# A low-rank product in transposed form, laid out by a DMA transpose, in a Fourier mixing and MLP kernel

## The chip, the cores and the metric

The kernel runs on one core of one Trainium2 chip. The time is the device time of one execution in microseconds (us); before the change it was measured in three runs. A core has five engines, each with its own instruction stream: TensorE (PE in the profile; PEld is its weight loads), VectorE (DVE), ScalarE (ACT), GpSimd (POOL) and SyncE (SP), which here issues DMAs only. TensorE multiplies a stationary operand ("weights", loaded by an instruction of its own) with a moving operand and writes to PSUM; ScalarE and VectorE move results from PSUM to SBUF.

## The reference

x has 8 batches of 3136 rows (n) and 256 columns (d). First the real part of a Fourier transform along both axes, then a low-rank mix along the rows and an MLP along the columns:

```
X   = real(fft(fft(x, axis=1), axis=2))          # (8, 3136, 256)
h   = X.transpose(0, 2, 1) @ U @ V               # U 3136 x 32, V 32 x 3136
u   = X + h.transpose(0, 2, 1)
out = u + relu(u @ w_ch1) @ w_ch2                # w_ch1 256 x 1024, w_ch2 1024 x 256
```

## The kernel before

Everything is kept with d on the partitions (two halves of 128, index `s`) and rows n along the free axis. The Fourier transform is done by folding x with its mirror images on VectorE (`fold`) and multiplying with cosine and sine tables on TensorE (`transform`, tiles `pt`, then `pst`). It yields the two halves of the transformed columns as `ST[b]["S"]` and `ST[b]["T"]`. Rows n and 3136 - n come from the same numbers with the two column halves exchanged, so only half of the rows, 1568 a batch, are walked explicitly.

These 8 x 1568 columns are cut into 25 chunks (`c`) of 512, across batch bounds; `pieces(c)` gives the batches in a chunk. For each chunk:

- `front(c, hf)`: the low-rank part `ph` (TensorE) plus S and T (VectorE) gives `u`, for the direct rows (hf 0) and the mirrored rows (hf 1). SyncE then issues a DMA transpose of `u` into `ut`, which is used when the output is put together; GpSimd makes small corrections `fx` from it.
- `direct(c, q)`: for four blocks j of the hidden layer, w_ch1 times u into four PSUM tiles `p1`; ScalarE applies relu and writes `h`.
- `mirrors(c, q)`: the same four PSUM tiles are turned into the hidden layer of the mirrored rows, without a full product. Two terms are added: `WD` (difference of the halves of w_ch1) times `uo` (S - T), and the low-rank term, `QF` times `DV` (difference of the direct and mirrored columns of V). Then relu again.
- `second_product(c, hf, t0)`: w_ch2 times `h`; VectorE adds `ut`, GpSimd adds `fx`, and `store` issues the DMA out.

`QF` is what the change is about. `lowrank(b)` computes the transform of the batch's product with U, as `ptt`; copies of it go to `TA` and `TX`, and for batches 1 to 7 SyncE issues a DMA transpose of `TX` into `TD[b % 2]` (L659). `TD` has d on the partitions, two halves s, and 128 columns: the 32 rank columns four times over. `hidden(b, hh)` multiplies it with w_ch1 (`W1`), with TD as the weights, 512 columns of the hidden layer at a time (L689):

```
mm(pt[:], TD[b % 2][:, s, :], W1[:, s, hh * CH:(hh + 1) * CH], start=(s == 0), stop=(s == 1))
nc.scalar.copy(QF[b % 2][:, hh * CH:(hh + 1) * CH], pt[:])
```

So `QF[b % 2]` is 128 x 1024: on each of the four groups of 32 partitions the same 32 x 1024 product. `mirrors` (L795) needs it so: each of its four blocks g takes its weights from partition group g, and the four matmuls of 32 rows run on four row groups of TensorE.

Batch 0 is prepared in the setup, with a transposed product on TensorE (`transposed`) in place of the DMA transpose, and its two calls of `hidden` (L1038, L1082) use a spare PSUM tile.

What sets the order: the main loop runs over the chunks and has six slots in each (`turn(c, 0)` to `turn(c, 5)`); the steps of the next batch's transform are put into slots by `transform(b)` (L857 to L881) and `put`. The matmuls, and the folds on VectorE, stay in the order of the program; the scheduler places the other engines' instructions. For batch 1 the list ends `rank + ch, q`: in one slot the low-rank product and the four `chan` steps, in the next (the last of chunk 2) both halves of `hidden`. Batch 1 begins in chunk 3, at column 32 of it. For batch 2, `q` takes the last two slots of its list; for later batches each step has its own slot, and the two halves of `hidden` are the last two of 15, the last of them in the last slot before the chunk in which the batch begins. In that chunk `mirrors(c, 0)` is the first to read the new `QF`.

Of the kernel before, what the change touches and what calls it, by code (L numbers as in the profile page):

```python
# [10 lines left out]
BF16 = mybir.dt.bfloat16  # L11
FP32 = mybir.dt.float32
# [4 lines left out]
P = 128  # L17
# [14 lines left out]
def kernel(  # L32
# [9 lines left out]
    nc = tc.nc  # L42
    B, S, D = x.shape
    R = moe_U.shape[1]
    H = moe_w_ch1.shape[1]
    JT = H // P
    HALF = S // 2
    CH = 512
# [3 lines left out]
    cpool = ctx.enter_context(tc.tile_pool(name="cpool", bufs=1))  # L52
    psum = ctx.enter_context(tc.tile_pool(name="psum", bufs=1, space=bass.MemoryType.PSUM))
# [51 lines left out]
    BUFS = {"dft": 2, "p1": 4, "p2": 2}  # L105
# [15 lines left out]
    def iota(out_, pattern, base, m=0):  # L121
# [8 lines left out]
                      in_=bass.AP(moe_U.tensor, moe_U.offset + R,  # L130
                                  [[NI * R, PQ], [784 * R, 4], [1, NI * R]]))
# [54 lines left out]
    W1 = cpool.tile([P, 2, H], BF16, name="w1")  # L186
# [3 lines left out]
    DV = cpool.tile([P, HALF], BF16, name="dv")  # L190
# [1 line left out]
    TA = [cpool.tile([P, 256], BF16, name=f"ta{s}", tag=f"ta{s}") for s in range(2)]  # L192
    TX = cpool.tile([P, 256], BF16, name="tx")
    TD = [cpool.tile([P, 2, P], BF16, name=f"td{s}", tag=f"td{s}") for s in range(2)]
    QF = [cpool.tile([P, H], BF16, name=f"qf{s}", tag=f"qf{s}") for s in range(2)]
    MSN = cpool.tile([P, 256], BF16, name="msn")
    MC = cpool.tile([P, 256], BF16, name="mc")
    MSX = cpool.tile([P, 256], BF16, name="msx")
# [251 lines left out]
    def mm(*a, **k):  # L450
        ins = nc.tensor.matmul(*a, **k)  # L451
        if len(pinned) > 1:
            tc.keep_in_program_order(ins)
        if pinned:
            pinned.append(ins)
# [68 lines left out]
    def seq(b, par, typ, pn, tag="dft", part=True):  # L524

        d = state(b)
        ne = NE if b else 0
        pt = psum.tile([P, QW], FP32, tag=tag, name="pt", bufs=BUFS[tag])
        d["pt"] = pt
        todo = products(b, par, typ, P * typ, pn == 1, ne)  # L530
        if typ == 0:
            todo = todo + products(b, par, 1, 256, (pn == 1) == (par == 1), ne)
        add_up(pt, todo)
        if pn == 0:
            ev = d["ev"] = wp.tile([P, QW], FP32, tag="ev", name="ev", bufs=EB)
            w = (2 * NT if par else TE) + ne
            nc.scalar.copy(ev[:, :w], pt[:, :w])
            if part:
                apart(b, par)
# [12 lines left out]
    def join(b, par, typ, kept=None, low=True, high=True):  # L552

        d = kept or ST[b]
        ne = NE if b else 0
        pt, ev = d["pt"], d["ev"]
        dst = ST[b]["A"] if typ == 1 else ST[b]["B"]
        p_, e_ = pt[:, 0:2 * NT], d["eh"][:]
        up, dn = dst[:, 1176:784:-1], dst[:, 1177:HALF + 1]
        if low:  # L560
            nc.vector.tensor_tensor(up, p_, e_, op=AL.add)
        if not high:
            return
        if typ == 1:
            nc.vector.tensor_tensor(dn, e_, p_, op=AL.subtract)
        else:
            nc.vector.tensor_tensor(dn, p_, e_, op=AL.subtract)
        if ne:
            pu, eu = 2 * NT, NT
            nc.vector.tensor_tensor(ST[b]["tab"][:, typ, par, :].rearrange("p (g r) -> p g r", r=R),  # L570
                                    four(pt, pu), four(ev, eu), op=AL.add)

    def even_rows(b, typ, pn, tag="dft"):

        d = state(b)
        ne = NE if b else 0
        if pn == 0:
            d["pe"] = psum.tile([P, QW], FP32, tag=tag, name="pt", bufs=BUFS[tag])
        pt = d["pe"]
        todo = products(b, 0, typ, P * typ, pn == 1, ne)  # L580
        if typ == 0:
            todo = todo + products(b, 0, 1, 256, pn == 0, ne)
        for n, (at, w, rhs) in enumerate(todo):
            mm(pt[:, at:at + rhs.shape[-1]], w, rhs, start=(pn == 0 and n == 0),
               stop=(n == len(todo) - 1), skip_group_check=True)
        if pn == 0:
            ev = d["ve"] = wp.tile([P, QW], FP32, tag="ev", name="ev", bufs=EB)
            nc.scalar.copy(ev[:, :TE + ne], pt[:, :TE + ne])
            return
        dst = d["A"] if typ == 1 else d["B"]  # L590
        nc.scalar.copy(strip(dst[:], 392, [[-2, NT + 1]]), pt[:, 0:NT + 1])
        nc.scalar.copy(strip(dst[:], 391, [[-2, NT]]), pt[:, NT + 1 + ne:TE + ne])
        if ne:
            nc.scalar.copy(d["tab"][:, typ, 0, :].rearrange("p (g r) -> p g r", r=R), four(pt, TE - NT))
# [7 lines left out]
    def mirrored(b, typ, kept):  # L602

        ne = NE if b else 0
        pt, ev = kept["pe"], kept["ve"]
        dst = ST[b]["A"] if typ == 1 else ST[b]["B"]
        nc.vector.scalar_tensor_tensor(strip(dst[:], 394, [[-1, 2], [2, NT]]),  # L607
                                       strip(ev[:], 1, [[NT + ne, 2], [1, NT]]), 2.0 if typ else -2.0,
                                       strip(pt[:], 1, [[NT + ne, 2], [1, NT]]),
                                       op0=AL.mult, op1=AL.subtract if typ else AL.add)  # L610
# [71 lines left out]
                   stop=(typ == 1))  # L682
        nc.scalar.copy(TD[b % 2][:], pt)

    def hidden(b, hh, spare=None):

        pt = spare or psum.tile([P, CH], FP32, tag="dft", name="pq", bufs=BUFS["dft"])
        for s in range(2):
            mm(pt[:], TD[b % 2][:, s, :], W1[:, s, hh * CH:(hh + 1) * CH], start=(s == 0), stop=(s == 1))  # L689
        nc.scalar.copy(QF[b % 2][:, hh * CH:(hh + 1) * CH], pt[:])  # L690

    def width(c):
        return min(CH, NCOL - c * CH)
# [1 line left out]
    def pieces(c):  # L695

        cuts = []
        r = c * CH
        while r < c * CH + width(c):
            b, n = divmod(r, HALF)  # L700
            end = min(c * CH + width(c) - b * HALF, HALF)
            cuts.append((b, n, end, r - c * CH))
            r = b * HALF + end
        return cuts
# [60 lines left out]
    def extent(c, hf):  # L765
        return width(c) + (B if hf == 0 and width(c) < CH else 0)
# [17 lines left out]
    def mirrors(c, q):  # L784

        k = CK[c]
        w = extent(c, 1)
        for g in range(4):
            j = 4 * q + g
            mm(k["p1"][g][:, :w], WD[:, j * P:(j + 1) * P], k["uo"][:, :w], start=False, stop=False,  # L790
               skip_group_check=True)
        for b, lo, hi, col in pieces(c):
            for g in range(4):
                j, rows = 4 * q + g, slice(g * R, (g + 1) * R)
                mm(k["p1"][g][:, col:col + hi - lo], QF[b % 2][rows, j * P:(j + 1) * P], DV[rows, lo:hi],  # L795
                   start=False, stop=True, skip_group_check=True)
        for g in range(4):
            nc.scalar.activation(k["h", 1][q][:, g, :w], k["p1"][g][:, :w][:, ::-1], AF.Relu)  # L798
# [58 lines left out]
    def transform(b):  # L857

        def odd_rows(typ, pn):
            seq(b, 1, typ, pn)  # L860
            if pn:
                join(b, 1, typ)

        def even(typ, pn):
            even_rows(b, typ, pn)
            if pn:
                mirrored(b, typ, ST[b])

        a = [lambda pn=pn: even(1, pn) for pn in range(2)]
        s = [lambda pn=pn: even(0, pn) for pn in range(2)]  # L870
        c = [lambda pn=pn: odd_rows(1, pn) for pn in range(2)]
        d = [lambda pn=pn: odd_rows(0, pn) for pn in range(2)]
        rank = [lambda: lowrank(b)]
        ch = [lambda ch=ch, h=h: chan(b, ch, h) for ch in range(2) for h in range(2)]
        q = [lambda hh=hh: hidden(b, hh) for hh in range(2)]
        if b == 1:
            return 11, [a[:1], a[1:] + c[:1], c[1:], [s[0], d[0]], [s[1], d[1]], rank + ch, q]
        if b == 2:
            return 23, [a[:1], a[1:] + c[:1], [], c[1:] + s[:1], s[1:], d[:1], d[1:], rank, ch[:1], ch[1:3],
                        ch[3:], q[:1], q[1:]]  # L880
        return 6 * (b * HALF // CH) - 15, [[x] for x in a + c + d[:1] + s + d[1:] + rank + ch + q]  # L881

    CK = {}
    ST = {}
# [146 lines left out]
    spare = psum.tile([P, CH], FP32, tag="p2", name="spare", bufs=BUFS["p2"])  # L1031
# [3 lines left out]
    nc.vector.tensor_tensor(WD[:], W1[:, 1, :], W1[:, 0, :], op=AL.subtract)  # L1035
    nc.gpsimd.memset(WD[0:1], 0.0)
    first_rows(0, 0, "dft")
    hidden(0, 0, spare)  # L1038
    setup.close()
    cp = ctx.enter_context(tc.tile_pool(name="cp", bufs=2))  # L1040
    front(0, 0)
# [37 lines left out]
    direct(0, 0)  # L1079
    chan(0, 2, 0)  # L1080
    chan(0, 2, 1)
    hidden(0, 1, spare)  # L1082
    mirrors(0, 0)
    front(0, 1)
    first_rows(0, 256, "p2")
# [4 lines left out]
    chan(0, 3, 1, "p2")  # L1090
    along_d(OD, xr, EOR_, 1)
    mirrors(0, 1)
    front(1, 0)
    alone(EV, xr, EOR_)
# [8 lines left out]
    for c in range(1, NCH):  # L1103
# [17 lines left out]
        if c + 1 < NCH:  # L1121
# [6 lines left out]
                      in_=CK[NCH - 1]["o", 0][:B, 2, :])  # L1128
# [32 lines left out]
```

## Time and profile before

| what | us |
|---|---|
| median of three runs | 456.95 |
| lowest, highest run | 455.19, 462.61 |
| profiled execution, its own time | 455.13 |
| its span, first to last instruction | 453.0 |
| TensorE matmul busy | 434.7 |
| VectorE, ScalarE, GpSimd busy | 314.5, 298.5, 121.5 |
| `pq` matmuls (the product `hidden`, batches 1 to 7), 28 of them, mean of one 0.379 | 8.2 |
| `qf` copies on ScalarE, 14 of them, mean of one 0.587 | 8.1 |

All numbers below the second line come from one profiled execution. In a timeline a row gives the start, the length, the engine, the line, and output<-inputs by tile name; the line of a matmul is that of the helper `mm` (L451), so matmuls are told apart by their tiles. A matmul's length contains its drain, which overlaps with the next one, so the price of a group of matmuls is read from its start to the start of what follows. `[idle before <-releaser]` at a row's end is the engine's idle time before it and what ended it. Rows of SyncE (SPq) give the time that the queue spent on issuing a DMA, not the time until the data landed; that is read from who waited for it, or from the completion marks in the trace, 16 for each transfer.

### The profile page before, as it was taken

How to read it: one execution, taken by the hardware profiler on the slowest of the kernel's cores; microseconds unless marked ns; L12 is line 12 of the kernel's file. 1: busy time of each engine (PE TensorE's matmuls, PEld its weight loads, DVE VectorE, ACT ScalarE, POOL GpSimd, SP SyncE). 2: the span in 40 equal slices, each digit the busy share in tenths (PEclk: the TensorE clock that was granted, in tenths of full speed). 3: DMA queues.
4: the chain of work that ended last, by engine and by line, in shares of the span. 5: the costliest groups of instructions: out<-in, count | busy, mean ns of one | idle time of the engine just before them, and what ended most of it. 6: DMA issues, size and time to landing. Idle time of an engine off the chain costs nothing.

```text
span 453.0 us, 9053 instructions
## 1 busy us (share of the span) xinstructions
PE 434.7 (96%) x3351; PEld 285.4 (63%) x3351; DVE 314.5 (69%) x639; ACT 298.5 (66%) x640; POOL 121.5 (27%) x338
## 2 busy tenths in 40 slices
PE   5989999999999999999999999999999999999995
PEld 2664666566666676667666666667666666666673
DVE  8898975995887768669667768579667444344442
ACT  7958755766567657765667657775667657765751
POOL 8970221341224224422133111321122000111010
PEclk9999999999999999999999999999999999999999
DMA  7996797769467683946878397774325423435463
GB/s 205 221 224 150 180 238 103 170 165 239 121 169 212 155 199 84 261 105 156 170 147 209 99 188 91 147 197 128 94 75 131 104 72 98 94 112 121 117 128 107
DMA packets 89132, 67.79 MB, mean 150 GB/s; under 512 B 55372, under 2 KB 82400, under 8 KB 89088
## 3 DMA queue, kind: packets, MB, share of 16 engines
q1 hardware_dynamic: 83608, 52.86, 51.3%
q0 software_dynamic: 5472, 14.36, 12.7%
q8 instruction: 26, 0.43, 0.4%
q14 instruction: 18, 0.15, 0.1%
q10 hardware_dynamic: 8, 0.00, 0.0%
HBM read 28.86 MB, written 25.69 MB: 120 GB/s over the span
## 4 chain that ended last, share of the span: by engine, by line
PE 84%; DVE 7%; DMA 4%; ACT 2%; issue 1%; SPq 1%; POOL 0%; DVEq 0%; POOLq 0%
PE p L451 64%; PE pt L451 10%; PE pst L451 4%; DMA xr<-in_x_dram 3%; PE ph L451 3%; PE pq L451 1%; DVE eof L446 1%; DVE u L737 1%; DVE A L607 1%; DVE eor L446 1%; PE ptt L451 1%; DVE go L446 1%; DMA out_dram<-o 1%; SPq L87 1%; DVE eos L446 0%
## 5 line engine op out<-in xcount | busy, mean ns | idle before, releaser
L451 PE MATMUL p<-w,h 128*128 128x256 bf16 x1576 | 189.1, 273 | 0.0
L451 PEld LDWEIGHTS <-h 128*128 128x128 bf16 x1576 | 149.6, 98 | 39.2 <-issue 17.4
L798 ACT ACTIVATE h<-p 128x512 bf16<-128x512 f32 (+1 forms) x200 | 101.6, 594 | 59.4 <-PE p L451 57.3
L782 ACT ACTIVATE h<-p 128x512 bf16<-128x512 f32 (+1 forms) x200 | 101.8, 600 | 7.3 <-PE p L451 7.3
L850 DVE TENSOR_TENSOR o<-p,ut 128x256 f32<-128x256 f32 x95 | 40.0, 421 | 91.4 <-PE p L451 72.8
L451 PE MATMUL p<-u,w 128*128 128x512 bf16 (+1 forms) x400 | 93.2, 375 | 0.6 <-DVE u L737 0.6
L855 POOL TENSOR_TENSOR o<-o,fx 128x2 f32<-128x2 f32 (+1 forms) x95 | 34.7, 365 | 135.0 <-DVE o L851 68.0
L451 PEld LDWEIGHTS <-w 128*128 128x128 bf16 x400 | 38.9, 98 | 39.8 <-issue 2.1
L451 PE MATMUL p<-uo,wd 128*128 128x512 bf16 (+1 forms) x200 | 50.8, 374 | 0.2
L57 POOL DMA_INDIRECT xf<-in_x_dram,xidx x32 | 38.7, 1210 | 20.8 <-DVE eof L446 9.6
L446 DVE TENSOR_TENSOR eor<-xr 99x1016 bf16<-99x1016 f32 x32 | 38.4, 1209 | 1.6 <-DMA xr<-in_x_dram 1.6
L851 DVE TENSOR_TENSOR o<-p,ut 128x256 f32<-128x256 f32 x95 | 39.3, 413 | 0.0
L446 DVE TENSOR_TENSOR eof<-xf 99x1016 bf16<-99x1016 f32 x32 | 38.2, 1208 | 0.2 <-issue 0.2
L737 DVE TENSOR_TENSOR u<-ph,T 128x512 bf16<-128x512 f32 (+8 forms) x64 | 35.0, 558 | 4.5 <-PE ph L451 2.8
L737 DVE TENSOR_TENSOR u<-ph,S 128x512 bf16<-128x512 f32 (+8 forms) x64 | 35.0, 558 | 0.9 <-PE ph L451 0.3
L755 POOL TENSOR_TENSOR fx<-ut 128x4 f32<-128x4 bf16 x48 | 11.7, 243 | 68.9 <-DMA ut<-u 68.9
L451 PEld LDWEIGHTS <-wd 128*128 128x128 bf16 x200 | 19.4, 97 | 16.7 <-issue 0.4
L754 POOL TENSOR_TENSOR fx<-ut 128x4 f32<-128x4 bf16 x24 | 6.6, 273 | 77.8 <-DMA ut<-u 72.5
L451 PE MATMUL pt<-te,gc 98*128 98x229 bf16 (+1 forms) x192 | 24.2, 260 | 1.8 <-DVE u L737 1.6
L451 PEld LDWEIGHTS <-go 98*128 98x128 bf16 x216 | 19.2, 97 | 10.2 <-issue 3.1
L645 ACT CAST T<-pst 128x392 bf16<-128x392 f32 (+1 forms) x28 | 17.4, 621 | 11.5 <-PE pst L451 11.5
L451 PEld LDWEIGHTS <-gc 98*128 98x128 bf16 x216 | 19.2, 97 | 6.4 <-issue 2.2
(167 smaller groups left out, 465.9 us busy)
## 6 DMA issues: line engine op xcount, KB each, us to landing
out_dram<-o SPq DMA_DIRECT2D x33, 512.0 KB
xr<-in_x_dram SPq DMA_DIRECT2D x16, 784.0 KB
out_dram<-o SPq DMA_DIRECT2D x8, 384.0 KB
out_dram<-o SPq DMA_DIRECT2D x9, 256.0 KB
out_dram<-o SPq DMA_DIRECT2D x8, 128.0 KB
ut<-u SPq DMA_TRANSPOSE x48
vv<-vv SPq DMA_DIRECT2D x3, 196.0 KB
out_dram<-o SPq DMA_DIRECT2D x6, 96.0 KB
```

What stands on the lines that cost most here:

```text
L57: nc.gpsimd.indirect_dma_start(out_, None, bass.AP(t.tensor, t.offset, [[w, rows], [1, w]]), bass.IndirectOffsetOnAxis(idx, 0), element_of ...
L446: ins = nc.vector.tensor_tensor(*a, **k)
L451: ins = nc.tensor.matmul(*a, **k)
L645: nc.scalar.copy(to, pt[:, :n])
L737: nc.vector.tensor_tensor(u[:, s, at:at + hi - lo], phs[s][:, at:at + hi - lo], src, op=AL.add)
L754: nc.gpsimd.tensor_tensor(fx[:, :, 0], ut[:, n:2 * n, 0], ut[:, 0:n, 0], op=AL.subtract)
L755: nc.gpsimd.tensor_tensor(fx[:, :, 1], ut[:, 0:n, 0] if hf else ut[:, n:2 * n, 0], ut[:, n + 1:2 * n + 1, 0], op=AL.subtract)
L782: nc.scalar.activation(k["h", 0][q][:, j - 4 * q, :w], p1[:, :w], AF.Relu)
L798: nc.scalar.activation(k["h", 1][q][:, g, :w], k["p1"][g][:, :w][:, ::-1], AF.Relu)
L850: nc.vector.tensor_tensor(o[:, ts, 0:P], p2[:, :w, 0:P], ut[:rows, ts, 0:P], op=AL.add)
L851: nc.vector.tensor_tensor(o[:, ts, P:D], p2[:, :w, P:D], strip(ut[:rows], (CH // P + t0 + 1) * P, [[P, w], [-1, P]]), op=AL.add)
L855: nc.gpsimd.tensor_tensor(o[:, ts, cols], o[:, ts, cols], fx[:rows, ts, 1 - hf:], op=AL.add)
```

## The change

For batches 1 to 7 the product is computed the other way round. `W1` gives the weights, block by block of 128 hidden columns, and the moving operand is the first of the four copies in `TD`, 32 columns. Eight blocks and two halves s make 16 matmuls into one PSUM tile of 128 x (8 x 32). One ScalarE copy puts it into `QT` (128 x 256), and one DMA transpose on SyncE's queue turns its two blocks of 128 x 128 into `QF[b % 2]`, now 128 x 2 x 128: block j = 4q + g lies on partition group g, at q. Each product is thus held once instead of four times. Batch 0 keeps the wide product (`hidden_0`) with a tile of its own, `QF0`, laid out by q, g, column. `mirrors` takes its weights from the one or the other. In the list of steps the product is now one step: in the same slot for batch 1, and ahead of the last `chan` steps for the others (ahead of one step of two for batch 2, ahead of two for batches 3 to 7, whose lists have 14 steps instead of 15).

```diff
-    QF = [cpool.tile([P, H], BF16, name=f"qf{s}", tag=f"qf{s}") for s in range(2)]
+    QF0 = cpool.tile([P, 2, 4, P], BF16, name="qf")
+    QF = [cpool.tile([P, 2, P], BF16, name=f"qf{s}", tag=f"qf{s}") for s in range(2)]
+    QT = cpool.tile([P, 2 * P], BF16, name="qt")
...
-    def hidden(b, hh, spare=None):
-
-        pt = spare or psum.tile([P, CH], FP32, tag="dft", name="pq", bufs=BUFS["dft"])
+    def hidden_0(hh, pt):
+
         for s in range(2):
-            mm(pt[:], TD[b % 2][:, s, :], W1[:, s, hh * CH:(hh + 1) * CH], start=(s == 0), stop=(s == 1))
-        nc.scalar.copy(QF[b % 2][:, hh * CH:(hh + 1) * CH], pt[:])
+            mm(pt[:], TD[0][:, s, :], W1[:, s, hh * CH:(hh + 1) * CH], start=(s == 0), stop=(s == 1))
+        nc.scalar.copy(QF0[:, hh].rearrange("p g m -> p (g m)"), pt[:])
+
+    def hidden(b):
+
+        pt = psum.tile([P, JT, R], FP32, tag="dft", name="pq", bufs=BUFS["dft"])
+        for j in range(JT):
+            for s in range(2):
+                mm(pt[:, j, :], W1[:, s, j * P:(j + 1) * P], TD[b % 2][:, s, 0:R], start=(s == 0), stop=(s == 1))
+        nc.scalar.copy(QT[:], pt[:].rearrange("p j r -> p (j r)"))
+        nc.sync.dma_start_transpose(out=QF[b % 2][:], in_=QT[:])
...
-                j, rows = 4 * q + g, slice(g * R, (g + 1) * R)
-                mm(k["p1"][g][:, col:col + hi - lo], QF[b % 2][rows, j * P:(j + 1) * P], DV[rows, lo:hi],
+                rows = slice(g * R, (g + 1) * R)
+                mm(k["p1"][g][:, col:col + hi - lo], QF0[rows, q, g, :] if b == 0 else QF[b % 2][rows, q, :], DV[rows, lo:hi],
...
-        q = [lambda hh=hh: hidden(b, hh) for hh in range(2)]
+        q = [lambda: hidden(b)]
...
-                        ch[3:], q[:1], q[1:]]
-        return 6 * (b * HALF // CH) - 15, [[x] for x in a + c + d[:1] + s + d[1:] + rank + ch + q]
+                        q, ch[3:]]
+        return 6 * (b * HALF // CH) - 15, [[x] for x in a + c + d[:1] + s + d[1:] + rank + ch[:2] + q + ch[2:]]
...
-    hidden(0, 0, spare)
+    hidden_0(0, spare)
...
-    hidden(0, 1, spare)
+    hidden_0(1, spare)
```

## The prediction

> **What bounds the kernel now.** I read the page first (share of the engines, chain of waits), then TensorE's timeline around the product that is changed, then the queue of SyncE and the landings of its transposes, then the granted clock by windows.
>
> ```profile
> span 453.0 us, 9053 instructions
> PE 434.7 (96%) x3351; PEld 285.4 (63%) x3351; DVE 314.5 (69%) x639; ACT 298.5 (66%) x640; POOL 121.5 (27%) x338
> PE   5989999999999999999999999999999999999995
> PE 84%; DVE 7%; DMA 4%; ACT 2%; issue 1%; SPq 1%; POOL 0%; DVEq 0%; POOLq 0%
> ```
>
> TensorE is busy in nearly every slice and carries 84% of the chain of waits. Its timeline shows no idle stretch over 0.1 us after 150 us, and only six over 0.2 us between 60 and 150 us. So time taken off TensorE's stream comes off the end one for one, and so does a wait put into it.
>
> The product that is changed, and what reads it, at the first batch that it touches (batch 1), in TensorE's timeline (start, duration, what):
>
> ```profile
> 84.44 1.03 PE L451 MATMUL pq<-w,td 128*128 128x512 bf16 x4
> 85.30 1.89 PE L451 MATMUL p<-u,w 128*128 128x512 bf16 x8
> 90.40 0.41 PE L451 MATMUL p<-dv,qf 32*128 32x32 bf16 x8
> ```
>
> The next product starts 0.86 us after the four wide matmuls, so that is their price (the 1.03 contains a drain that overlaps). The last line is the first use of batch 1's `qf` (eight matmuls: four narrow ones of batch 0, from 90.44 four of batch 1): 5.96 us after the product began.
>
> **The matmuls.** Seven batches (1 to 7) change; batch 0 keeps its form (`hidden_0`). Removed: 4 matmuls of 512 columns, 0.86 us a batch. Added: 16 of 32 columns, each with its own 128-column weight load. The nearest row is the low-rank product of the setup, also 32 columns on 128-column weights:
>
> ```profile
> 26.36 0.35 PE L451 MATMUL ptu<-te,gc 98*128 98x32 bf16 x8
> ...
> 26.77 0.35 PE L451 MATMUL ptu<-te,gc 98*128 98x32 bf16 x8
> ...
> 27.17 0.85 PE L451 MATMUL pt<-te,gc 98*128 98x197 bf16 x8
> ```
>
> 32 such matmuls stand between 26.36 and 27.17: 25 ns each, so 16 take 0.40 us. A farther row bounds it from above: the `pu` matmuls, with weights only 98 columns wide, run 12 in 0.54 us (12.28 to 12.82), 45 ns each, 0.72 us for 16. From below 0.40 is the fastest in the trace. I take 0.40: same width of weights. Gain 0.46 us a batch, 3.2 us in all (1.0 us at the other bound).
>
> [...]
>
> **The evictions.** ScalarE loses two `qf` copies of 0.586 us and gets one of 128x256: 0.37 us by the `tx` copy of the same shape. ScalarE is 66% busy and idles 0.4 to 1.2 us ahead of those copies; no gain on the path, no loss. One bank of the two-buffer `dft` pool is taken per batch instead of two; the trace has no wait for it at this place: nothing.
>
> **The transposes.** Seven transposes of 128x256 go on SyncE's queue. Their shape is that of `td<-tx` (1.17 to 1.97 us of queue time). Behind them wait the x loads and output stores of that stage; the folds that read those loads come at least a chunk (some 16 us) later, so 1.2 us there costs nothing. What matters is when they land, since TensorE now waits for them at the mirror products. Landing is not instant, even when issued at once: by the trace's completion marks (last of 16) `td` landed 2.3, 2.4, 2.7, 3.6, 4.1, 2.3 and 2.3 us after the start of its issue. In six of the seven a `ut` transpose was still in flight when `td` was issued, and `td` always landed after it, by 0.26 to 0.55 us in the three slow ones (177.58 then 178.13; 228.90 then 229.16; 282.96 then 283.44): the queue hands on in order.
>
> In the changed program each new transpose stands right behind a `ut` transpose on SyncE, except for batch 2, where two small loads lie between. At batch 1:
>
> ```profile
> 84.49 5.36 SPq L751 DMA_TRANSPOSE ut<-u  x1
> 89.90 0.43 SPq L87 DMA_DIRECT2D xr<-in_x_dram  x1
> ```
> ```profile
> 96.43 0.54 POOL L755 TENSOR_TENSOR fx<-ut 128x4 f32<-128x4 bf16 x1 [6.39 <-DMA ut<-u]
> ```
>
> The first view is SyncE's queue, the second is GpSimd. SyncE is held by this `ut` transpose until 89.85, while 784 KB of x, a 512 KB store and two gathers are in the queues (DMA share 0.91 from 84 to 97 us); the transpose's data are complete at 96.35 (marks of 14 engines by 95.45), which is when GpSimd goes on. The new transpose issues at 89.9, so its bounds are: 92.2 if it lands 2.3 us after issue as on an idle queue, 96.6 to 96.9 if it lands behind the `ut` one. I take 96.7, by those three rows. TensorE comes to its use at 90.44 - 0.46 = 89.98. All that is queued behind is TensorE itself, in program order: the mirror products, the next low-rank products and second products, and with them every eviction. It resumes at 96.7 against 90.44: **+6.3 us** (the first 0.46 is swallowed).
>
> Some of it is absorbed. VectorE was itself late there (it evicts the next `ph` at 92.24 although the product ended at 91.0), so the gaps of 0.22 and 0.53 us that TensorE has at 93.1 and 101.2, the second waiting on VectorE, close: -0.8. Bounds: 0, and -2.1 if the later gaps at 120.0 (0.87) and 145.7 (0.46) close too.
>
> Batches 2 to 7, TensorE's need against the landing that I expect, in the old times: batch 2 142.8 against 135.3; batch 3 194.3 against 189.0; batch 4 245.1 against 239.8; batch 5 296.06 - 0.46 = 295.6 against 295.06 + 0.4 = 295.5; batches 6 and 7 over 9 us spare. No wait, but batch 5 has none to spare: 0, bound +0.5.
>
> **The earlier place.** From batch 2 on the product moves ahead of chan steps, so `td` is needed sooner: in batch 5 at 282.62 (where the third `chan` stood) instead of 286.76, and `td` landed there at 283.44: +0.8 (0 to 1.3). In the other batches `td` is 2.6 us or more early.
>
> **The clock.** A stop of 6.7 us has a price of its own:
>
> ```profile
> 444.00:452.80 8.80, 3.60 (x32) 2.55 (x29) 1.99 (x6) 0.22 (x1) 1.09 (x6) 1.00 0.37 122
> 452.90:453.00 0.10, 0.00 (x0) 0.00 (x0) 0.00 (x0) 0.00 (x0) 0.00 (x0) 0.50 0.00 0
> ```
>
> The windows give TensorE's granted clock third from the end: 1.00 up to 452.8, then 0.50. The last matmul ends at 447.60 and the clock record falls at 452.87: 5.3 us of rest halve it. At the start the first matmul is at 5.23 and full clock is recorded from 9.14: 3.9 us to come back. A stop of 6.7 us is longer than 5.3, so I count half speed over 3.9 us: +1.9 (0 if the stop is cut under 5.3).
>
> [...]
>
> **Sum.** +6.3 - 6 x 0.46 (2.8) + 1.9 + 0.8 - 0.8 = +5.4 us on the profiled execution, whose own time is 455.13 (span 453.0, 2.1 around it): 460.5. The median of the three runs is 456.95, 1.8 above; on that footing I forecast **461.5**, 1.0% slower.
>
> **Rivals.**
> *The wait stays short.* If the new transpose lands at 92.2, TensorE resumes 1.8 us late, the clock holds, and +1.8 - 2.8 + 0.4 (half of batch 5's) - 0.4 gives -1.0: 455.9. If nothing waits anywhere, -3.2: 453.7. For it: `td` lands 2.3 us after issue four times of seven. Against: no `td` landed before a `ut` transpose that was in flight ahead of it. Chance 0.17.
>
> *The wait repeats (slower).* Place: batch 5's mirror product. Its `ut` transpose took 7.4 us from issue to landing; the ones issued at 62.37 and 84.49 took 11.9. If, with work bunched behind the first stop, batch 5's takes 11.9 as well, `qf` lands at 300.0 against 295.6: +4.4, with the clock's 1.9 another 6.3 at most, so 466.7 to 468.6; batches 3 and 4 would join once theirs land 5.2 us later. It decides from 3.7 us of further wait, since 2% is 9.1 us. For it: no margin in batch 5, and waits of this queue double under load. Against: by then stores and loads are steady. Chance 0.24.
>
> *The narrow matmuls are slower than 25 ns.* At 45 ns, 7 x 0.32 = +2.2: 463.7. [...] Chance 0.06.
>
> *It gains over 2%.* The four wide matmuls of seven batches total 6.0 us (1.3%); even free they don't reach 9.1. Chance 0.02, for something that I don't see.
>
> The forecast itself has 0.51, with its own range 458 to 464.5. The range that leaves out no more than 2 in 10 goes from 453.7 (nothing waits) to 468.6 (the repeat). Faster or slower by over 2%, about what runs of this kernel can tell (455.19 to 462.61 before), is 447.8 and 466.1: faster 0.02; slower 0.25, the repeat and a little of the slow matmuls; the rest, 0.73, within.
>
> **What would show it.** In the changed profile: the 16 matmuls at 25 ns (about 0.4 us to the next product); an idle stretch of TensorE of about 6.7 us ahead of `p<-dv,qf` near 90 us, ended by the DMA of `qf`; a granted clock under 1.00 for some 4 us after it; no such stretch before 280 us; a short one near 282 us, ended by `td`. I am wrong if `qf` lands well before 95 us, if the same stretch comes back in batches 3 to 5, or if the clock stays whole through the stop.

## The result, and the profile after

The changed kernel takes 463.69 us (median of five runs, 461.22 to 465.37) against 456.93 for the kernel before on the same chip. The ratio is 1.0145, with an interval of 1.0104 to 1.0186: about 1.5% slower. The profiled execution took 463.69 us.

The page of the changed kernel, the lines that answer to those of before (span; busy times; TensorE and its granted clock in 40 slices; the chain of waits):

```profile
span 461.8 us, 9236 instructions
...
PE 434.9 (94%) x3435; PEld 286.6 (62%) x3435; DVE 314.3 (68%) x639; ACT 294.2 (64%) x633; POOL 125.9 (27%) x338
...
PE   5989999739999999999999999999999999999995
...
PEclk9999999959999999999999999999999999999998
...
PE 86%; DMA 6%; DVE 4%; ACT 2%; SPq 1%; issue 1%; DVEq 0%; POOLq 0%
```

TensorE's row has two slices that are not full, 7 and 3, and the clock's row a 5 in the second of them. Everything else looks as before. The span grew by 8.8 us, and one place holds more than that. TensorE's timeline there, and further on, at batches 2 and 5:

```profile
84.25 0.55 PE L453 MATMUL pq<-td,w 128*128 128x32 bf16 x16
84.66 1.89 PE L453 MATMUL p<-u,w 128*128 128x512 bf16 x8
...
89.75 0.19 PE L453 MATMUL p<-dv,qf 32*128 32x32 bf16 x4
99.47 0.59 PE L453 MATMUL p<-dv,qf 32*128 32x480 bf16 x4 [9.53 <-DMA qf<-qt]
...
100.42 3.54 PE L453 MATMUL p<-w,h 128*128 128x256 bf16 x16
...
148.64 1.67 PE L453 MATMUL p<-u,w 128*128 128x512 bf16 x7 [0.27 <-DVE u L747]
...
293.17 0.56 PE L453 MATMUL pq<-td,w 128*128 128x32 bf16 x16 [0.61 <-DMA td<-tx]
```

The sixteen narrow matmuls cost 0.41 us (84.25 to 84.66), against 0.86 before. At 89.75 the four matmuls of batch 0 run from `QF0`; the next four, the first of batch 1, wait 9.53 us for the transposition. The 16 second products behind them take 3.54 us instead of 1.9. SyncE's queue shows what came before:

```profile
84.30 6.33 SPq L761 DMA_TRANSPOSE ut<-u  x1
90.72 1.19 SPq L700 DMA_TRANSPOSE qf<-qt  x1
```

By the completion marks `ut` landed at 98.98 and `qf` at 99.43: issued at 90.72, it took 8.7 us. The windows of the stage (columns: stretch; its length; busy time of PE, PEld, DVE, ACT and POOL; granted clock; DMA share; GB/s):

```profile
84.00:93.50 9.50, 5.95 (x56) 3.75 (x54) 7.57 (x12) 3.97 (x8) 1.51 (x2) 1.00 1.01 203
93.60:103.70 10.10, 4.22 (x24) 2.58 (x25) 1.55 (x6) 2.07 (x4) 1.80 (x6) 0.50 0.75 141
103.90:110.00 6.10, 6.10 (x48) 3.58 (x46) 5.05 (x9) 3.63 (x8) 3.53 (x6) 1.00 0.65 176
```

The clock is 0.50 from 93.5 to 103.8, the last 4.3 us of it after TensorE has resumed, and the DMA engines are full (share 1.01) up to 93.5. TensorE's list of waits gives the new transposition once only:

```profile
PE p L453 <- DMA qf<-qt: 9.5, 1, 9.5
...
PE pq L453 <- DMA td<-tx: 0.6, 1, 0.6
```

To see where the rest went, the start of each mirror product (its first `p<-uo,wd` matmul) was compared between the two traces. After minus before, in us:

| from | to | after minus before | what lies there |
|---|---|---|---|
| start | batch 1's product | -0.18 | |
| batch 1's product | the stop | -0.65 | the product, -0.46 |
| the stop | batch 2's product | +10.68 | +11.33: 9.53 idle, the rest clock |
| batch 2's use | batch 3's product | +10.74 | the gain of batch 2 is missing |
| batch 3 | batch 4 | +10.24 | -0.44 |
| batch 4 | batch 5 | +9.78 | -0.46 |
| batch 5's `td` wait | behind it | +10.53, then +10.09 | +0.75, then -0.44 |
| batch 6, batch 7 | end | +9.63, +9.17 | -0.46 each |
| end of the span | | +8.78 | |

At batch 2 the earlier TensorE meets VectorE, which evicts `u` too late for it: the gap of 0.27 at 148.64 in the timeline above, which the kernel before did not have, and about 0.2 ahead of the matmul before that. So the 0.43 us of batch 2 are not gained.

### The profile page after: what moved, and what is told of

Same layout as the page of the kernel before. It is cut to its first block, busy times and chain, and to the rows that moved or that the text cites. A ratio compares the mean times of both kernels' runs of the same rounds, so it can differ in the third digit from the quotient of the medians.

```text
span 461.8 us, 9236 instructions
## 1 busy us (share of the span) xinstructions
PE 434.9 (94%) x3435; PEld 286.6 (62%) x3435; DVE 314.3 (68%) x639; ACT 294.2 (64%) x633; POOL 125.9 (27%) x338
## 4 chain that ended last, share of the span: by engine, by line
PE 86%; DMA 6%; DVE 4%; ACT 2%; SPq 1%; issue 1%; DVEq 0%; POOLq 0%
PE p L453 67%; PE pt L453 10%; PE pst L453 4%; DMA xr<-in_x_dram 3%; PE ph L453 3%; DMA qf<-qt 2%; DVE u L747 1%; DMA td<-tx 1%; DVE A L609 1%; DVE eor L448 1%; PE ptt L453 1%; PE pq L453 1%; SPq L87 1%; ACT h L808 0%; ACT h L792 0%
## 5 line engine op out<-in xcount | busy, mean ns | idle before, releaser
L865 POOL TENSOR_TENSOR o<-o,fx 128x2 f32<-128x2 f32 (+1 forms) x95 | 37.1, 391 | 154.7 <-DVE o L861 86.4
L453 PEld LDWEIGHTS <-w 128*128 128x128 bf16 x512 | 41.7, 97 | 39.5 <-issue 2.6
L765 POOL TENSOR_TENSOR fx<-ut 128x4 f32<-128x4 bf16 x48 | 12.9, 270 | 62.6 <-DMA ut<-u 62.6
L453 PE MATMUL p<-dv,qf 32*128 32x512 bf16 (+15 forms) x256 | 19.9, 336 | 9.5 <-DMA qf<-qt 9.5
L764 POOL TENSOR_TENSOR fx<-ut 128x4 f32<-128x4 bf16 x24 | 7.1, 296 | 68.8 <-DMA ut<-u 68.8
```

The lines of the kernel that those rows point to most:

```text
L764: nc.gpsimd.tensor_tensor(fx[:, :, 0], ut[:, n:2 * n, 0], ut[:, 0:n, 0], op=AL.subtract)
L765: nc.gpsimd.tensor_tensor(fx[:, :, 1], ut[:, 0:n, 0] if hf else ut[:, n:2 * n, 0], ut[:, n + 1:2 * n + 1, 0], op=AL.subtract)
L865: nc.gpsimd.tensor_tensor(o[:, ts, cols], o[:, ts, cols], fx[:rows, ts, 1 - hf:], op=AL.add)
```

## The experiments

Ratios are against the kernel before, run beside it on the same chip, with their intervals. Shifts are taken as in the table above. Unless said otherwise the diffs are against the changed kernel. "The stop" is TensorE's wait at batch 1's mirror product.

### Taking the stop away

**Batch 1 keeps the wide product** (`QF0` and `QF1` are its tiles and serve batches 2 to 7 as well):

```diff
-    QF = [cpool.tile([P, 2, P], BF16, name=f"qf{s}", tag=f"qf{s}") for s in range(2)]
+    QF1 = cpool.tile([P, 2, 4, P], BF16, name="qfw")
+    QF = [t[:, 0, 0:2, :] for t in (QF0, QF1)]
...
+    def hidden_1(hh):
+        pt = psum.tile([P, CH], FP32, tag="dft", name="pq", bufs=BUFS["dft"])
+        for s in range(2):
+            mm(pt[:], TD[1][:, s, :], W1[:, s, hh * CH:(hh + 1) * CH], start=(s == 0), stop=(s == 1))
+        nc.scalar.copy(QF1[:, hh].rearrange("p g m -> p (g m)"), pt[:])
...
-            return 11, [a[:1], a[1:] + c[:1], c[1:], [s[0], d[0]], [s[1], d[1]], rank + ch, q]
+            return 11, [a[:1], a[1:] + c[:1], c[1:], [s[0], d[0]], [s[1], d[1]], rank + ch,
+                        [lambda hh=hh: hidden_1(hh) for hh in range(2)]]
```

> Batch 1 alone goes back to the wide product without a transpose; batches 2 to 7 stay changed. If the loss is TensorE's wait for batch 1's transpose: no idle stretch near 90 us, clock 1.00 throughout, the later batches keep their gain of about 0.45 us each and batch 5 its wait of 0.6 us: 6 x 0.45 - 0.6, so 2.1 us under the kernel before (ratio 0.995). If the seven transposes cost something by being in the queue (six remain), it stays slower than before, by over 4 us.

Measured: 454.15 us, ratio 0.9945 (0.9904 to 0.9986), clock 1.00 throughout. The place of the stop, in TensorE's timeline of this kernel:

```profile
90.31 0.20 PE L454 MATMUL p<-dv,qf 32*128 32x32 bf16 x4
90.35 0.37 PE L454 MATMUL p<-dv,qfw 32*128 32x480 bf16 x4
```

The second four follow at once. From batch 3 on the shift falls by 0.44 to 0.47 a batch, as in the changed kernel. Batch 5's wait for `td`, which was to stay, is absent in this profile and there again (0.4 us) in the next one. The same kernel was run again later beside other kernels:

> The kernel with batch 1 alone in the wide form a second time, beside the two above. If its gain is real: ratio 0.993 to 0.997 again; if the first ratio came from the spread between runs, its interval now holds 1.

Measured: 453.08 us, ratio 0.9943 (0.9909 to 0.9977). So the one transposition of batch 1 carries the whole loss, and the six others with their narrow products are a gain. In the first of the two profiles the shift also rose by 1.1 us near 106 us, where VectorE could not write an output tile until its earlier store had landed:

```profile
105.77 0.42 DVE L868 TENSOR_TENSOR o<-p,ut 128x256 f32<-128x256 f32 x1 [4.09 <-DMA out_dram<-o]
```

TensorE lost 0.95 us at 106.91 by that; this one was not in the second profile. In the first profile the DMA share was 1.01 from 84 to 97 us and 0.62 from 97 to 104; that the crowded stage made the earlier store late as well is an estimate from these shares, and was not shown.

**The transposition stays, nothing waits for it.** The mirror products of batch 1 read batch 0's tile:

```diff
-                mm(k["p1"][g][:, col:col + hi - lo], QF0[rows, q, g, :] if b == 0 else QF[b % 2][rows, q, :], DV[rows, lo:hi],
+                mm(k["p1"][g][:, col:col + hi - lo], QF0[rows, q, g, :] if b < 2 else QF[b % 2][rows, q, :], DV[rows, lo:hi],
```

> The changed kernel, in which the mirror products of batch 1 read batch 0's product (the mirrored rows of batch 1 get a wrong low-rank term); batch 1's narrow product, its copy and its transpose are still issued at the same place. If the wait alone is the loss: 7 x 0.45 - 0.6, so 2.5 us under the kernel before (ratio 0.9945). If issuing the transpose into the full queue delays something else too, the time stays over the kernel before.

Measured: 452.55 us, ratio 0.9885 (0.9817 to 0.9953, from four runs; the forecast 0.9945 lies within). The transposition was issued at 89.38 and landed at 98.52, as late as in the changed kernel, and cost nothing. It is the wait that costs, not the traffic of the transposition.

**The transposes alone**, added to the kernel before (diff against it) with nobody reading them:

```diff
+    QX = cpool.tile([P, 2, P], BF16, name="qx")
...
         nc.scalar.copy(QF[b % 2][:, hh * CH:(hh + 1) * CH], pt[:])
+        if b and hh == 0:
+            nc.sync.dma_start_transpose(out=QX[:], in_=QF[b % 2][:, 0:2 * P])
```

> The kernel before plus the seven transposes of the same shape on SyncE's queue, issued after the first half of each wide product, into a tile that nobody reads. If transposes in the queue cost nothing unless waited for: ratio 1.000, within 0.5 us. If they hold up loads, stores or the transposes of u: slower by several us, with new idle stretches of TensorE.

Measured: 455.23 us, ratio 0.9955 (0.9918 to 0.9991). From 37 us on the shift is constant, -0.43 to -0.47 us up to the last stage: no transposition moved anything. The ratio below 1 can't come from work that was added, and the trace's small lead lies wholly ahead of the first of them; it shows that a ratio here can be off by some 0.4%, with 1 outside its interval, which the verdicts here have to bear.

### What the clock costs

**TensorE is kept busy ahead of the wait**, with 40 matmuls whose result nobody reads:

```diff
         for b, lo, hi, col in pieces(c):
+            if c == 3 and q == 0 and b == 1:
+                pf = psum.tile([P, CH], FP32, tag="dft", name="fill", bufs=BUFS["dft"])
+                for _ in range(40):
+                    mm(pf[:, 0:2 * NT], TABO[0][:PQ, 0, 1, 0:P], TABO[0][:PQ, 0, 0, 0:2 * NT], start=True, stop=True)
```

> The changed kernel with 40 matmuls of 392 columns (40 x 0.165 = 6.6 us), whose result nobody reads, put on TensorE ahead of the stretch in which it waits for batch 1's transpose. If half clock after the stop is a price of its own: the clock stays 1.00, the transpose lands when it did (97 to 99.5 us), and the time is 1.8 us under the changed kernel, ratio to before about 1.0105. If the clock costs nothing by itself, the ratio stays at 1.0145; if the filler itself is too long, it is higher.

Measured: 460.04 us, ratio 1.005 (1.0013 to 1.0086), clock 1.00 throughout. TensorE's timeline of this kernel:

```profile
89.19 6.81 PE L453 MATMUL fill<-to 98*128 98x392 bf16 x40
98.79 0.38 PE L453 MATMUL p<-dv,qf 32*128 32x480 bf16 x4 [2.79 <-DMA qf<-qt]
...
99.33 1.92 PE L453 MATMUL p<-w,h 128*128 128x256 bf16 x16
```

The time without useful work is the same, 9.60 us (89.19 to 98.79) against 9.53, but the 16 products behind it take 1.92 us instead of 3.54. The shift jumps by 9.31 us here and by 11.33 in the changed kernel: the clock's part of the loss is 2.0 us. The ratio fell by more than the 1.8 us that were forecast (1.0105, outside the interval); it was taken beside the same runs of the kernel before as that of the transposes alone, which came out 0.4% low as well, so the clock's part is read from the traces.

### What sets the landing

**The transposition ahead of `ut`.** The low-rank product of batch 1 goes before `front(3, 0)`, so that SyncE issues `qf` before the `ut` transpose that held it:

```diff
-            return 11, [a[:1], a[1:] + c[:1], c[1:], [s[0], d[0]], [s[1], d[1]], rank + ch, q]
+            return 11, [a[:1], a[1:] + c[:1], c[1:], [s[0], d[0]], [s[1], d[1]], rank + ch, []]
...
         mirrors(c, 1)
+        if c == 2:
+            hidden(1)
```

> The changed kernel with batch 1's product moved ahead of front(3, 0), so that SyncE issues its transpose before the ut transpose of chunk 3 and not behind it; nothing else is moved. If the transpose is late because it stands behind that ut transpose in the queue: it lands between 87 and 91 us, TensorE's wait falls from 9.5 to 0 to 2 us, with at most 0.5 us of a new wait for td; 1 to 2.5 us under the kernel before (ratio 0.9945 to 0.998). If the load on the DMA engines as a whole sets the landing, whatever the order: it lands at 95 us or later and 5 us or more of the wait stay, ratio over 1.003.

Measured: 463.88 us, ratio 1.0179 (1.0146 to 1.0212): no better. SyncE's queue, and TensorE, in this kernel:

```profile
85.11 2.12 SPq L700 DMA_TRANSPOSE qf<-qt  x1
87.32 4.78 SPq L761 DMA_TRANSPOSE ut<-u  x1
```
```profile
85.06 0.59 PE L453 MATMUL ph<-vv,ta 32*128 32x32 bf16 x3 [1.74 <-ACT qt L699]
...
100.51 0.58 PE L453 MATMUL p<-dv,qf 32*128 32x480 bf16 x4 [6.58 <-DMA qf<-qt]
```

`qf` was issued 5.6 us earlier than in the changed kernel and landed at 100.47, 1.0 us later than the changed kernel's had (99.43). Being first on its queue didn't help: it took 15.4 us. An early place on SyncE's queue is therefore not enough. Two things were new. TensorE waited 1.74 us at 85.06, because the next product needs a PSUM tile that ScalarE's `qt` copy had to free first. And GpSimd issued its next two gathers of x at 86.51 and 87.80; in the kernel before they come at 89.06 and 97.16, the second behind `fx`, which waits for `ut`. So more was in flight while `qf` was, and what the order alone would do is not shown here.

**The same, and a later place for the product in batches 3 to 7** (one `chan` step behind it instead of two):

```diff
-        return 6 * (b * HALF // CH) - 15, [[x] for x in a + c + d[:1] + s + d[1:] + rank + ch[:2] + q + ch[2:]]
+        return 6 * (b * HALF // CH) - 15, [[x] for x in a + c + d[:1] + s + d[1:] + rank + ch[:3] + q + ch[3:]]
```

> The same, and for batches 3 to 7 the product one step later (behind three chan steps, not two). SyncE then issues the transpose behind the 784 KB x load that follows ut. The wait for td in batch 5 (0.5 us) goes. If the margin of batch 5 is as thin as the prediction had it, its transpose now lands 3 us later, at some 295 us, and TensorE waits there for 0.5 to 3 us; if there is margin to spare, the time is 0.5 us under that of the run before it in this list.

Measured: 464.96 us, ratio 1.0223 (1.0176 to 1.027). At batch 5 the wait for `td` is gone, and one for `qf` has come in its place:

```profile
306.00 0.33 PE L453 MATMUL p<-dv,qf 32*128 32x352 bf16 x4 [0.45 <-DMA qf<-qt]
```

In the changed kernel batch 5's transposition had landed at 303.81, 2.3 us ahead of its use at 306.15. The later place used up this margin and a little more: what it gains on one side it loses on the other.

Three kernels then take bytes out of the stage. They are for the landing, not for the time.

**Without one store** of 512 KB, issued just ahead of the `ut` transpose:

```diff
-        store(c - 1, 1)
+        if c != 2:
+            store(c - 1, 1)
```

> The changed kernel without one output store of 512 KB, the one that SyncE issues just ahead of the ut transpose near 84 us (the mirrored rows of chunk 1 are not written). If the queue of bytes ahead sets the landing of batch 1's transpose: 512 KB at the 200 GB/s of that stretch are 2.5 us, so it lands at 95.5 to 97 us and the wait is 6.5 to 8 us; at under 5.3 us the clock would hold too. If the two transposes themselves take the time, the wait stays at 9 us or more.

**Without one load** of 784 KB (x of batch 3), which SyncE issues ahead of that store:

```diff
-        load_r(x, xr, b, 1 - nm, 2, D)
+        if (b, nm) != (3, 0):
+            load_r(x, xr, b, 1 - nm, 2, D)
```

> The changed kernel without one 784 KB load of x, the one that SyncE issues near 83 us (batch 3 is folded with rows of batch 2 in its place). Leaving out the 512 KB store let batch 1's transpose land 6.4 us earlier, 12.5 ns for each KB. If bytes ahead count alike, whatever they are: 9 us or more, so it lands by 90 us and the wait is under 0.7 us. If what counts is the number of small packets (the store's are of 1 KB, the load's of 4 KB): it gains less than the store did, and the wait stays at 3.5 us or more.

**Without two gathers** of x of batch 3 on GpSimd's own queue (99 x 1016 x 4 bytes, 402 KB, each by the shape of the tile that is read from it):

```diff
-        for q in (0, 2) if nm == 0 else (1, 3):
+        for q in () if (b, nm) == (3, 0) else (0, 2) if nm == 0 else (1, 3):
```

> The changed kernel without the two gathers of x (400 KB each, 4 KB packets) that GpSimd issues near 81 and 82 us on its own queue (batch 3 again is folded with rows of batch 2). If bytes on the other queue hold up SyncE's queue as its own do: batch 1's transpose lands 6 us or more earlier and the wait is under 4 us. If only what stands ahead in SyncE's own queue counts: it lands when it did, within 1.5 us, and the wait stays at 8 us or more.

Measured, one execution each. Since the stage starts up to 2 us earlier or later from run to run, the times from issue to landing are the ones to compare:

| kernel | time SyncE spent on `ut` | `ut`, issue to landing | `qf`, issue to landing | the stop |
|---|---|---|---|---|
| changed kernel | 6.33 | 14.7 | 8.7 | 9.53 |
| without the store | 2.56 | 8.5 | 6.4 | 3.30 |
| without the load | 2.64 | 6.4 | 4.0 | 1.17 |
| without the gathers | 1.25 | 6.2 | 5.3 | 1.91 |

The stops, in TensorE's timelines of the kernels without the store, the load and the gathers, in this order:

```profile
93.09 0.59 PE L453 MATMUL p<-dv,qf 32*128 32x480 bf16 x4 [3.30 <-DMA qf<-qt]
```
```profile
92.98 0.38 PE L453 MATMUL p<-dv,qf 32*128 32x480 bf16 x4 [1.17 <-DMA qf<-qt]
```
```profile
91.22 0.38 PE L453 MATMUL p<-dv,qf 32*128 32x480 bf16 x4 [1.91 <-DMA qf<-qt]
```

The times were 456.8, 454.6 and 454.47 us (456.27 for the kernel before). Each of the three, the gathers of another engine's queue too, shortens the stop by 6 to 8 us. The forecasts for the store (a wait of 6.5 to 8 us) and for the load (under 0.7 us, or 3.5 and more) were missed; for the gathers the first of the two came. The store did more than the 2.5 us that its share of the bytes would give, but each of these kernels also moved another transfer. GpSimd's next gather of x starts at 88.86 in the changed kernel, 4.6 us behind the issue of `ut`; without the store and without the load it came at 92.98 and 93.77, after `ut` had landed. First the changed kernel's GpSimd, then that of the kernel without the load:

```profile
88.86 0.99 POOL L57 DMA_INDIRECT xf<-in_x_dram,xidx  x1 [1.99 <-DVE eof L448]
```
```profile
93.77 0.99 POOL L57 DMA_INDIRECT xf<-in_x_dram,xidx  x1 [0.18 <-DVE eor L448]
```

Without the gathers the store went out 2.4 us ahead of `ut` instead of 0.5. So the table shows that the landing follows the traffic in flight; what a single transfer is worth was not separated. With two gathers fewer on GpSimd's queue the `ut` transposition on SyncE's landed 8.5 us sooner after its issue (6.2 us against 14.7); how the DMA engines divide their time between the queues was not shown. An early place on SyncE's queue gave no early landing in the kernel with `qf` ahead of `ut`, where it took 15.4 us instead of 8.7.

**The loads held back.** The changed kernel, in which the loads of x for batch 3 wait, those on SyncE until the transposition of `qf` has been issued, the gathers on GpSimd until the `fx` of chunk 3 that needs `ut`.

```diff
+    HOLD = {}
+
     def load_part(b, nm):
+        with ExitStack() as behind:
+            if b == 3:
+                for ins in HOLD.values():
+                    behind.enter_context(tc.issue_after(ins))
+            load_now(b, nm)
+
+    def load_now(b, nm):
...
-        nc.sync.dma_start_transpose(out=QF[b % 2][:], in_=QT[:])
+        ins = nc.sync.dma_start_transpose(out=QF[b % 2][:], in_=QT[:])
+        if b == 1:
+            HOLD["sp"] = ins.ins
...
-        nc.gpsimd.tensor_tensor(fx[:, :, 1], ut[:, 0:n, 0] if hf else ut[:, n:2 * n, 0],
+        ins = nc.gpsimd.tensor_tensor(fx[:, :, 1], ut[:, 0:n, 0] if hf else ut[:, n:2 * n, 0],
...
+        if (c, hf) == (3, 0):
+            HOLD["pool"] = ins.ins
...
-            spread_out(list(fold(b)), lo, mid)
+            steps_f = list(fold(b))
+            held = [steps_f.pop(4)] if b == 2 else []
+            spread_out(steps_f, lo, mid)
+            put(20, *held)
```

> The changed kernel, complete, with the x loads of batch 3 held back in the stage of the wait: SyncE issues the 784 KB load only behind batch 1's qf transpose, GpSimd its gathers only behind the fx of chunk 3 (that is, once that ut transpose has landed). Nothing is left out. If the bytes in flight set the landing: ahead of it are a 512 KB store and the ut transpose alone, so it lands by 91 us (leaving out either load alone gave 91.2 and 92.9), the wait is 0 to 1.5 us, the clock holds, and the time is 1 to 2.5 us under the kernel before (ratio 0.9945 to 0.998). If the loads then come too late for batch 3's folds, a new idle stretch of TensorE stands between 100 and 140 us and takes it back.

Measured: 452.57 us (twelve runs, 451.07 to 454.5), ratio 0.993 (0.9901 to 0.9958), clock 1.00 throughout. SyncE's queue, and TensorE, in this kernel:

```profile
83.57 1.58 SPq L773 DMA_TRANSPOSE ut<-u  x1
85.25 1.20 SPq L710 DMA_TRANSPOSE qf<-qt  x1
86.50 0.43 SPq L87 DMA_DIRECT2D xr<-in_x_dram  x1
86.99 0.35 SPq L76 DMA_DIRECT2D xr<-in_x_dram  x1
```
```profile
89.19 0.41 PE L453 MATMUL p<-dv,qf 32*128 32x32 bf16 x8
89.43 0.39 PE L453 MATMUL ph<-vv,ta 32*128 32x32 bf16 x4
```

The `ut` transpose holds SyncE for 1.58 us instead of 6.33, `qf`, still behind `ut` on its queue, lands at 87.59, 2.3 us after its issue, and the eight matmuls at 89.19 stand in one row: no stop. The 512 KB store also went out earlier here, 2.5 us ahead of `ut` instead of 0.5, so a part may be owed to its place. The loads, now some 4 us later on SyncE, cause no new wait; the folds that read them come later.

Its control holds the same loads back in the kernel before:

> The control: the kernel before with the same loads held back (on SyncE behind the ut transpose of chunk 3). If the loads are moved at no cost: ratio 1.000, within 0.5 us. If TensorE was also waiting for something that these loads delayed: faster by itself, and the run above owes that part to the move and not to the narrow product.

```diff
-        nc.sync.dma_start_transpose(out=ut[:, 0:2 * n], in_=u.rearrange("p s r -> p (s r)"))
+        sp = nc.sync.dma_start_transpose(out=ut[:, 0:2 * n], in_=u.rearrange("p s r -> p (s r)"))
...
+            HOLD["pool"] = ins.ins
+            HOLD["sp"] = sp.ins
```

Measured: 456.28 us, ratio 0.9995 (0.9966 to 1.0024). Holding the loads is worth nothing by itself. In the changed kernel it turns 1.0145 into 0.993, since there TensorE waits for what the loads delay. This version beats the kernel before by 0.7%; its interval and that of the wide batch 1 (0.9943) overlap, so which of the two is the better one stays open.

## Why the prediction was right, and where it was off

It forecast 461.5 us, with 458 to 464.5 as that case's own range, and 463.69 came. The mechanism was the one named, at the place named, and once; the loss was larger because one term of the sum was too small. On the spans the sum was +5.4 us, and +8.8 was measured. The number came closer than the sum. From the median of 456.95 us, +5.4 makes 462.4 and not 461.5: the forecast lost 0.9 us in its last step, and its rivals start partly from the one and partly from the other. And on the medians the loss is 6.8 us; the profiled execution before was 1.8 us under its median, so a part of the 8.8 belongs to this pair of executions.

- **The matmuls.** Forecast 0.40 us for sixteen, from the setup's 32-column row; measured 0.41 us, 25.6 ns each, and a shift of -0.44 to -0.46 in six batches (forecast 0.46). The rival of slower matmuls did not come: at the 45 ns of the setup's `pu` row it makes 463.7, inside the 2%, and no run shows a matmul of this shape slow enough for the little that it was given beyond. Batch 2 gained nothing, since VectorE's `u` was late there: +0.5 that was not in the sum. The gap of 0.46 at 145.7, taken as something that might close, showed how near VectorE is at that place.
- **The evictions, the queue time of the transposes.** Forecast at nothing; the kernel with transposes alone and the one without the wait show that they are (ratios 0.9955 and 0.9885).
- **The landing at batch 1: the term that was mis-sized.** Forecast: resume at 96.7, +6.3 us with the 0.46 of the narrow product taken off. Measured: resume at 99.47 after a stop of 9.53 us, +9.1 us in the same terms. The step was "the transposition lands behind `ut`, and `ut` lands at 96.35". Its first half held: `qf` came 0.45 us behind `ut` in the changed kernel, and 0.3 to 0.5 in five others. Its second half took one execution's landing for the landing. In the runs in which the traffic of that stage was left as it was, the same `ut` transpose landed this long after its issue: 11.3 and 11.9 (transposes alone, and the kernel before), 12.3 and 13.5 (batch 1 wide, twice), 14.0 (no wait), 14.7 (changed kernel) and 14.8 us (kept busy). The prediction had the second shortest of the seven. Whether the three longest, all with the narrow product, are longer by the change or by chance stays open; the transposes behind `ut` aren't the cause, since the shortest has them too. In all seven the gather that GpSimd issued 4.6 us behind `ut` landed within 0.7 us of it; no run changed that gather alone.
- **Absorption.** Forecast -0.8: the gaps of 0.22 and 0.53 close. Measured -0.2. The 0.22 closed; the 0.53 is still there (0.535 at 111.90). VectorE reads what TensorE makes, so it was held up by the same stop (8.86 us of waiting for `ph`, up to 100.52) and was as late behind it as before.
- **The clock.** Forecast +1.9; measured 2.0 by the kernel that keeps TensorE busy, and the record shows half clock for 4.3 us after the stop, which at half speed is 2.15. There was luck in the size: its two figures, 5.3 us of rest and 3.9 us to come back, were one execution's. In this stop the clock fell after 3.6 us (89.95 to 93.54), and over the traces the rest at the end lasts 2.0 to 5.3 us and the return at the start 3.6 to 6.9. The condition that a stop under 5.3 us costs nothing failed: after 1.91 us (without the gathers) and 3.30 (without the store) the clock was halved.
- **Batches 2 to 7.** Forecast no wait for `qf`; there was none. Batch 5, forecast with 0.1 us to spare, had 2.3 (303.81 against 306.15); one step later it was late by 0.45 us.
- **The earlier place in batch 5.** Forecast +0.8 for `td`; measured 0.75 in the shift, 0.61 as the wait, at 293.17, which is the forecast's 282 plus the 10 us of delay.

The terms that differ: the stop +2.8, absorption +0.6, batch 2 +0.5, clock +0.1; against that the start of the run -0.2 and its end -0.4. That makes +3.4, the difference between 8.8 and 5.4.

Of the rivals, the short wait would have needed `qf` on an idle queue; with the loads held back it is just that (2.3 us from issue to landing), so the mechanism was real, and the load in flight decided against it. The repeat at batch 5 did not come: its landing moved with the work, not towards it.

## What to carry to other kernels

Before a product's layout is handed to a DMA transposition, take its landing in the fullest stage in which the bounding engine will wait for it, over several executions, and add a stop's price in clock (2.0 us here); the issue time says little, since `qf` landed 2.3 to 15.4 us after its issue in these kernels. If it lands late, moving it forward on its own queue may not help (15.4 us here, instead of 8.7): look on all queues for the bulk transfers in flight that nobody needs soon, and hold them until it is on its way (2.3 us here). One late transfer among seven decided the sign here, so look at each place by itself before the whole change is given up.

## What was not expected of the hardware

- **Bytes on another queue count too.** Without two gathers on GpSimd's queue a transposition on SyncE's landed 6.2 us after its issue instead of 14.7, and held SyncE for 1.25 us instead of 6.33. (The store on SyncE's own queue also stood 1.9 us further ahead of it in that run.)
- **The clock fell after stops far shorter than the 5.3 us at the end of the run, and in steps of 3.41 us.** Half clock was recorded for 3.41 us after stops of 1.74 us (`qf` ahead of `ut`), 1.91 (without the gathers) and 3.30 (without the store); for 6.83 us around the stops of 6.58 and 7.00, and for 10.24 us around the one of 9.53. A stop of 1.73 us in the kernel with the later place, one of 1.17 without the load, and one of 2.79 behind the 40 matmuls that kept TensorE busy left it whole. The recorded lengths are one, two and three times 3.41 us, and the same length of stop went either way (1.73 us whole, 1.74 us halved). In the second profile with batch 1 wide a stop of 1.73 us in the setup halved the clock too, from 23.74 to 27.15, and that execution stood 1.2 to 1.3 us behind the kernel before from there to batch 3: a part of the spread between executions has nothing to do with the change. At half speed a step of 3.41 us costs a busy TensorE up to 1.7 us, an estimate (half of the 3.41), as much as the short stop that set it off; without the gathers the 16 second products behind the stop took 3.48 us instead of 1.92.
